# The upper feature half of the second expert, for two of four batches, goes from direct products to two added block steps; sums of x for the other two batches move into the attention

## The chip, the cores and the metric

The kernel runs on one core of a Trainium2 chip. The metric is the device time of one execution in microseconds, as the median of several executions. TensorE multiplies, VectorE, ScalarE and GpSimd work on the results, SyncE's queue issues most transfers.

## The reference

A gated linear attention gives the x of a mixture of experts, whose gate is balanced over all tokens:

```python
# q, k, v, f_logit: 4 batches, 8 heads, 768 steps, 48 wide
f = 1.0 / (1.0 + np.exp(-f_logit))
for t in range(S):
    state = f[:, :, t, :, None] * state + np.einsum('bhd,bhe->bhde', k[:, :, t], v[:, :, t])
    y[:, :, t] = np.einsum('bhd,bhde->bhe', q[:, :, t], state)
# x: y as 3072 tokens of 384; w1: 8 x 384 x 1024, w2: 8 x 1024 x 384
P = np.exp(x @ w_gate - max)
for _ in range(8):
    P /= P.sum(1, keepdims=True) + 1e-09
    P /= P.sum(0, keepdims=True) + 1e-09
    P *= N / E
for e in range(8):
    out += P[:, e:e + 1] * (np.maximum(x @ w1[e], 0.0) @ w2[e])
```

## The kernel before

Every product is made of f16 high and low parts, three matmuls for one. Tokens come in eight units u of 384; batch b holds units 2b and 2b+1. The experts are worked in two ways.

**Raw.** Experts 0 and 1 are multiplied directly. `moe(e, u, w)` makes, for each of `FT` = 8 feature tiles, nine matmuls of 384 columns into `hps`, which ScalarE turns into `hh` (relu, high part) and VectorE into `hl` (low part); then, for each of three token tiles, 24 matmuls of 384 columns into `yps`, which ScalarE copies to `yr` and SyncE writes to scratch. That is 72 + 72 matmuls for one expert and unit. `moe_tile` is the form for the first units, by token tile. Raw matmuls are TensorE's filler: `fill(n)` issues n of them between the steps of the attention (loop over g, amounts in `FILL`), and afterwards `LEAD` of them for each step of the balancing.

**The balancing** (`balance`, `sinkhorn`) is a serial chain of eight iterations, VectorE's row sums `sk_rs`, column sums `sk_cs` and products into `pe`, with one small matmul `sk_c` in each; that matmul is handed to TensorE's row `held_mm`, among the raw ones. In the same loop generators in `work` are advanced one step at a time: `convert(b)` and, from step `KSTEP` on, `prepare_w1` for the first block weights. `CONVSTEP` has the steps at which the next `convert` joins.

**Block.** Experts 2 to 7 use a scheme with fewer products: sums of blocks of x and of the weights, 15 block products for the first layer (`kb_A` to `kb_F`) and 7 for the second (`kyps`, `kxps`). A step ("period") is one entry (expert, half of the features, batch) of `ORDER`, 90 matmuls of 256 columns and 126 of 192; a group of four steps shares its weights. There are 48. `convert(b)` makes the batch's operands: three adds of high and low part (`x`), 17 sums on GpSimd (`XSUMS`, tile `xs`), copies (`XONE`), and five pieces of a split into f16 (ScalarE `xah`, `xbh`; VectorE `xal`, `xbl`). `prepare_w1` and `prepare_w2` do it for weights (`k1s` ten sums and `k2s` four on GpSimd, `k1h` and `k2h` on ScalarE, `k1l` and `k2l` on VectorE). `first_maxima`, `guard` and `verdict` look at the range of the inputs.

What sets the order: TensorE's instructions and, on VectorE, ScalarE and GpSimd, those that go through `pin` stand in the order in which the program writes them. Each engine takes its instructions in that order, and waits at the first one that isn't ready. `hps` and `yps` share four PSUM banks.

Of the kernel before, what the change touches and what calls it, by code (L numbers as in the profile page):

```python
# [1520 lines left out]
```

## Time and profile before

| | us |
|---|---|
| median of three runs | 1471.51 (1471.35 to 1471.69) |
| the profiled execution | 1472.94 |
| its span, first to last instruction | 1471.2 |
| TensorE busy | 1444.3 |
| VectorE busy | 1231.7 |
| ScalarE busy | 1061.0 |
| GpSimd busy | 1037.9 |

The profiled execution is 1.43 us above the median, and 1.74 us of it lie outside the span. Times of the trace are counted from the start of the span. The attention lasts to about 370 us, the balancing to 436, raw products to 483; then come the 48 block steps.

### The profile page before, as it was taken

The page shows a single profiled execution, that of the slowest core. Times are in us where ns is not written, and L with a number is a line of the kernel's source. Part 1 is how long each engine was busy: PE and PEld are TensorE (multiplying, and loading weights), DVE is VectorE, ACT ScalarE, POOL GpSimd, SP SyncE. Part 2 cuts the span into 40 slices and gives each one's busy share as a digit, 9 for nine tenths or more (in the row PEclk, how much of TensorE's full clock was granted, in tenths as well). Part 3 has the DMA queues.
Part 4 walks back from the last instruction along what each step waited for, and adds up shares of the span by engine and source line. Part 5 has one row for each costly group of instructions (what it writes and reads, how often), then busy time and mean ns, then how long its engine had stood idle before and what let it go on. Part 6 is the DMA issues. An engine that isn't in the chain of part 4 may idle for free.

```text
span 1471.2 us, 40349 instructions
## 1 busy us (share of the span) xinstructions
PE 1444.3 (98%) x16049; PEld 1258.5 (86%) x16049; DVE 1231.7 (84%) x2518; ACT 1061.0 (72%) x2380; POOL 1037.9 (71%) x1220
## 2 busy tenths in 40 slices
PE   7999999999999999999999999999999999999997
PEld 4788886666666799999999999999999999999996
DVE  7878888886686799888999999888888888888776
ACT  6756666664344777888888888888877787778764
POOL 2143434445457666999999999999998888888763
PEclk8999999999999999999999999999999999999999
DMA  8365455551001101222111111111111100000012
GB/s 250 101 144 136 117 126 137 130 111 55 16 34 33 49 12 29 62 61 61 56 55 53 53 57 39 48 50 55 50 34 34 34 27 30 14 20 14 2 55 79
DMA packets 107095, 92.77 MB, mean 63 GB/s; under 512 B 74160, under 2 KB 93744, under 8 KB 106896
## 3 DMA queue, kind: packets, MB, share of 16 engines
q1 hardware_dynamic: 106464, 89.51, 22.5%
q8 instruction: 127, 2.08, 0.6%
q14 instruction: 72, 0.59, 0.1%
q10 hardware_dynamic: 432, 0.59, 0.1%
HBM read 64.03 MB, written 14.16 MB: 53 GB/s over the span
## 4 chain that ended last, share of the span: by engine, by line
PE 91%; DVE 5%; ACT 2%; issue 1%; DMA 0%; POOL 0%; DVEq 0%; POOLq 0%; ACTq 0%
PE kyps L306 28%; PE yps L306 14%; PE hps L306 12%; PE kb_A L306 8%; PE kb_B L306 8%; PE kb_D L306 6%; PE kxps L306 5%; PE kb_C L306 4%; PE kb_E L306 2%; PE kb_F L306 2%; PE aps L306 1%; PE kvps L306 1%; ACT cp L1354 0%; DVE acc L1233 0%; DVE w1l L378 0%
## 5 line engine op out<-in xcount | busy, mean ns | idle before, releaser
L306 PEld LDWEIGHTS <-k1h 128*128 128x128 f16 x2880 | 270.8, 98 | 22.9 <-issue 3.9
L306 PE MATMUL kyps<-k2h,kgh 128*128 128x192 f16 x1152 | 283.4, 246 | 0.5 <-ACT kyps L1230 0.3
L306 PE MATMUL kyps<-k2l,kgh 128*128 128x192 f16 x1152 | 283.4, 246 | 0.0
L306 PE MATMUL kyps<-k2h,kgl 128*128 128x192 f16 x1152 | 283.4, 246 | 0.0
L306 PEld LDWEIGHTS <-kgh 128*128 128x128 f16 x2304 | 212.1, 98 | 7.3 <-issue 1.0
L1403 POOL TENSOR_TENSOR kgl<-kf,kgh 128x512 f16<-128x512 f32 x141 | 190.1, 1348 | 2.1 <-ACT kgh L1400 2.1
L1233 DVE SCALAR_TENSOR_TENSOR yy<-kyps,pes,part 128x192 f32<-128x192 f32 x258 | 106.5, 413 | 90.8 <-PE kyps L306 80.3
L1403 POOL TENSOR_TENSOR kgl<-kr,kgh 128x512 f16<-128x512 f32 x141 | 174.4, 1237 | 10.9 <-ACT kgh L1400 10.8
L1272 POOL TENSOR_TENSOR acc<-acc,yy 128x384 f32<-128x384 f32 x129 | 129.0, 1000 | 56.3 <-DVE yy L1233 56.3
L306 PEld LDWEIGHTS <-k1l 128*128 128x128 f16 x1440 | 140.9, 98 | 16.3
L306 PE MATMUL yps<-w2h,hl 128*128 128x384 f16 x384 | 125.3, 326 | 0.9 <-DVE hl L459 0.9
L306 PE MATMUL yps<-w2h,hh 128*128 128x384 f16 x384 | 125.3, 326 | 0.5 <-ACT hh L456 0.5
L306 PEld LDWEIGHTS <-w1h 128*128 128x128 f16 x1344 | 97.2, 98 | 33.1 <-issue 1.8
L306 PE MATMUL yps<-w2l,hh 128*128 128x384 f16 x384 | 125.3, 326 | 0.0
L306 PEld LDWEIGHTS <-kh 128*128 128x128 f16 x1152 | 108.3, 98 | 8.8 <-issue 2.5
L306 PEld LDWEIGHTS <-hh 128*128 128x128 f16 x768 | 74.1, 98 | 45.4 <-ACT hh L456 0.7
L306 PEld LDWEIGHTS <-kgl 128*128 128x128 f16 x1152 | 112.7, 98 | 0.2 <-issue 0.2
L1230 ACT ACTIVATE kyps<-kyps 128x192 f32<-128x192 f32 x144 | 45.7, 317 | 81.5 <-PE kyps L306 77.7
L1400 ACT ACTIVATE kgh<-kf 128x512 f16<-128x512 f32 x144 | 91.9, 638 | 1.0 <-DVE kf L1377 0.9
L1400 ACT ACTIVATE kgh<-kr 128x512 f16<-128x512 f32 x144 | 91.6, 636 | 0.0
L1354 ACT ACTIVATE cp<-kb_A 128x512 f32<-128x512 f32 x144 | 86.3, 599 | 3.1 <-DVE kb_A L1356 2.4
L410 DVE SCALAR_TENSOR_TENSOR hl<-hps,hh 128x384 f16<-128x384 f32 x80 | 44.0, 551 | 49.7 <-ACT hh L409 49.1
(300 smaller groups left out, 5278.1 us busy)
## 6 DMA issues: line engine op xcount, KB each, us to landing
q<-in_qkf_dram SPq DMA_DIRECT2D x23, 672.0 KB, 5.5
k1r<-in_w_dram SPq DMA_DIRECT2D x24, 384.0 KB, 3.0
ys<-yr SPq DMA_DIRECT2D x48, 192.0 KB, 2.2
k2r<-in_w_dram SPq DMA_DIRECT2D x24, 384.0 KB, 3.1
yb<-ys SPq DMA_DIRECT2D x48, 192.0 KB, 2.3
vr<-in_vc_dram SPq DMA_DIRECT2D x24, 192.0 KB, 4.9
out_dram<-acc SPq DMA_DIRECT2D x21, 192.0 KB, 1.9
w1r<-in_w_dram SPq DMA_DIRECT2D x8, 384.0 KB, 5.3
```

The lines of the kernel that those rows point to most:

```text
L306: ins = (nc.tensor.transpose if transpose else nc.tensor.matmul)(**kw)
L410: held[0] = pin(nc.vector.scalar_tensor_tensor(out=tl, in0=ps, scalar=0.0, in1=th, op0=ALU.max, op1=ALU.subtract))
L1230: pin(nc.scalar.activation(out=out, in_=in_, func=AF.Copy, **kw))
L1233: pin(nc.vector.scalar_tensor_tensor(out=y, in0=ps, scalar=p, in1=z, op0=ALU.mult, op1=ALU.add))
L1272: pin(nc.gpsimd.tensor_tensor(out=y, in0=y, in1=z.rearrange("p s d -> p (s d)"), op=ALU.add))
L1354: pin(nc.scalar.activation(out=fresh(ev[2]), in_=bk, func=AF.Copy))
L1400: pin(nc.scalar.activation(out=hs['g', t][0][i], in_=hs['f' if i else 'r', t], func=AF.Copy))
L1403: pin((nc.vector if tag == str(PERIODS - 1) else nc.gpsimd).tensor_tensor(out=hs['g', t][1][i], in0=hs['f' if i else 'r', t], in1=hs['g', ...
```

## The change

- Expert 1's upper 512 features, for the units 4 to 7 (`BLOCKED`, batches 2 and 3), are no longer raw: `features(e, u)` is 4 there and not 8. `ORDER` gets (1, 1, 2) and (1, 1, 3) at its end, a last group of two steps. The raw units are worked in the order of u, both experts for each.
- `convert` of batches 0 and 1 starts during the attention (`CONV0AT`), with its three adds on GpSimd; batch 0's is finished there, batch 1's splits come at the start of the balancing. Batches 2 and 3 join at the steps 18 and 40, with the adds on VectorE; what is left of batch 3 is spread over block step 0 (`CONVAT`), where before it was over step 1.
- `LEAD` is 7, `KSTEP` 12. An iteration of the balancing still has five steps; one small multiplication on VectorE is merged into another.
- x's maxima are not taken in `convert`: its high part is written to scratch, and `first_maxima` reads it back during the block steps. Weights in `UNSEEN` are looked at there too.
- The pools of `x32`, `xs` and the accumulators are split in two (`acca`, `accb`), and the block weights' pool opens earlier.

```diff
-RAW = [(e, u) for u in range(5) for e in range(2)] + [(0, 5), (0, 6), (0, 7), (1, 5), (1, 6), (1, 7)]
+RAW = [(e, u) for u in range(8) for e in range(2)]
+BLOCKED = (2, 3)
...
+ORDER = [(e, m, b) for e in range(2, NE) for m in range(2) for b in range(B)] + [(1, 1, b) for b in BLOCKED]
...
-LEAD = 8
+LEAD = 7
 FIRSTAT = ((0,), (1,), (0, 4), (0, 7), (1, 9), (5, 10))
 SECONDAT = ((16, 17), (18, 20), (17, 18), (17, 21), (20, 21), (20, 22), (24, 24), (23, 25))
-CONVSTEP = (26, 55, 70)
-KSTEP = 35
+CONVSTEP = (18, 40)
+KSTEP = 12
+CONV0AT = tuple(range(70, 206, 3))
...
-        yield
         pin(nc.vector.tensor_tensor(out=pe, in0=pe, in1=rs[:, :, None].to_broadcast([128, NT, NE]), op=ALU.mult))
+        yield
         pin(nc.vector.tensor_reduce(out=cs, in_=pe.rearrange("p a e -> p e a"), axis=AX.X, op=ALU.add))
         yield
         ps = psp.tile([128, NE], F32, name=f"sk_c{it}", tag=tag)
+        yield
         yield lambda: mm(out=ps, lhsT=onesf, rhs=cs, start=True, stop=True)
-        pin(nc.vector.tensor_scalar(out=cs, in0=ps, scalar1=1e-9, scalar2=None, op0=ALU.add))
+        pin(nc.vector.tensor_scalar(out=cs, in0=ps, scalar1=1e-9, scalar2=float(NE / N), op0=ALU.add, op1=ALU.mult))
         pin(nc.vector.reciprocal(out=cs, in_=cs))
-        pin(nc.vector.tensor_scalar(out=cs, in0=cs, scalar1=float(N / NE), scalar2=None, op0=ALU.mult))
-        yield
...
 
+    xscr = dp.tile([B, 128, KT, 2 * HS], F16, name="xscr")
...
+    tiles, put_off, owed = [0], [False], []
+
+    def features(e, u):
+        return FT // 2 if e and u // 2 in BLOCKED else FT
+
...
+    xc, xq = {}, []
+
+    def raw_tile(name):
+        return rp.tile([128, 768], F32, name=name, tag="wraw", bufs=3)
+
+    def convert(b):
+        xh, xl = xt[b]
+        if not all((u, t) in ready for u in (2 * b, 2 * b + 1) for t in range(TT)):
+            raise RuntimeError("a batch is not there")
+        nc.sync.dma_start(out=xscr[b], in_=xh.rearrange("p k u t -> p k (u t)"))
+        if b < 2:
+            x32 = [raw_tile(f"x32_{b}_{k}").rearrange("p (u t) -> p u t", u=2) for k in range(KT)]
+        else:
+            x32 = (acca, accb)[b % 2 == 0].tile([128, KT, 2, HS], F32, name=f"x32_{b}", tag="acc")
+            x32 = [x32[:, k] for k in range(KT)]
+        for k in range(KT):
+            pin((nc.gpsimd if b < 2 else nc.vector).tensor_tensor(out=x32[k].rearrange("p u t -> p (u t)"), in0=xh[:, k].rearrange("p u t -> p (u t)"), in1=xl[:, k].rearrange("p u t -> p (u t)"), op=ALU.add))
+            yield
...
+        yield
+        for i, (r, p, op, q) in enumerate(XSUMS):
+            pin(nc.gpsimd.tensor_tensor(out=block(r), in0=block(p), in1=block(q), op=ALU.add if op == '+' else ALU.subtract))
+            if i % 2:
+                yield
+        while b and not xq:
+            yield
+        xb = [(xq[0] if b else xq0).tile([128, 6, 256], F16, name=f"xb{n}{b}") for n in "hl"]
+        for n, (r, q, sign) in enumerate(XONE):
+            for src, dst in zip((xh, xl), xb):
+                pin(nc.scalar.activation(out=dst[:, 4 + n, :].rearrange("p (u t) -> p u t", u=2), in_=src[:, q // 3, :, 128 * (q % 3):128 * (q % 3) + 128], func=AF.Copy, scale=sign))
+            yield
+        while not {2 * b, 2 * b + 1} <= set(finished):
+            yield
+        xa = [xp.tile([128, 9, 256], F16, name=f"xa{n}{b}", tag=f"x{n}{b}", bufs=1) for n in "hl"]
...
+        if g in CONV0AT:
+            next(early, None)
         g += 1
+    for _ in converts[0]:
+        pass
...
+    work = [early]
     step, held_mm = 0, None
-    while True:
-        more = fill(LEAD * 5 / 8)
+    while fill(LEAD * 5 / 8):
         if held_mm:
             held_mm()
...
+        if not fill(LEAD * 3 / 8):
             break
         held_mm = next(chain, None)
         for gen in list(work):
@@ -1170,7 +1183,7 @@
                 work.remove(gen)
         step += 1
         if step in CONVSTEP:
-            work.append(converts[1 + CONVSTEP.index(step)])
+            work.append(converts[2 + CONVSTEP.index(step)])
...
-    at_all(1, CONVAT, converts[3])
+    at_all(0, CONVAT, converts[3])
```


Three places show how instructions move. The first is GpSimd during the balancing, where the sums of the second block weight tile (`k1s_1`) are made; `k2s_0` belongs to the first second-layer tile, `x_2` and `xs_2` to batch 2. Before:

```order
L1076 TENSOR_TENSOR k1s_1_8014<-k1r_1_8003 128x128 x2
L1076 TENSOR_TENSOR k1s_1_8014<-k1r_1_8003,k1s_1_8014 128x128
L1076 TENSOR_TENSOR k1s_1_8014<-k1s_1_8014,k1r_1_8003 128x128
L1076 TENSOR_TENSOR k1s_1_8014<-k1r_1_8003,k1s_1_8014 128x128
L1076 TENSOR_TENSOR k1s_1_8014<-k1s_1_8014 128x128
L1076 TENSOR_TENSOR k1s_1_8014<-k1r_1_8003,k1s_1_8014 128x128 x2
L1076 TENSOR_TENSOR k1s_1_8014<-k1s_1_8014,k1r_1_8003 128x128
L1076 TENSOR_TENSOR k1s_1_8014<-k1r_1_8003,k1s_1_8014 128x128
L1106 TENSOR_TENSOR k2s_0_8566<-k2r_0_8538 128x192 x2
L1109 TENSOR_TENSOR k2s_0_8566<-k2r_0_8538,k2s_0_8566 128x192 x2
L1021 TENSOR_TENSOR xs_2_8174<-x_2_8133 128x256 x2
```

With the change:

```order
L977 TENSOR_TENSOR xs_2_7671<-x_2_7626 128x256 x2
L977 TENSOR_TENSOR xs_2_7671<-xs_2_7671,x_2_7626 128x256
L977 TENSOR_TENSOR xs_2_7671<-x_2_7626 128x256
L1103 TENSOR_TENSOR k1s_1_7710<-k1r_1_7696 128x128 x2
L1135 TENSOR_TENSOR k2s_0_8194<-k2r_0_8162 128x192 x2
L1103 TENSOR_TENSOR k1s_1_7710<-k1r_1_7696,k1s_1_7710 128x128
L1138 TENSOR_TENSOR k2s_0_8194<-k2r_0_8162,k2s_0_8194 128x192
L1103 TENSOR_TENSOR k1s_1_7710<-k1s_1_7710,k1r_1_7696 128x128
L1138 TENSOR_TENSOR k2s_0_8194<-k2r_0_8162,k2s_0_8194 128x192
L1103 TENSOR_TENSOR k1s_1_7710<-k1r_1_7696,k1s_1_7710 128x128
L977 TENSOR_TENSOR xs_2_7671<-x_2_7626 128x256
L977 TENSOR_TENSOR xs_2_7671<-xs_2_7671,x_2_7626 128x256
```

The ten sums of `k1s_1` stood together and ahead of batch 2's; now the first four `xs_2` sums stand ahead of them, and the four of `k2s_0` and two more `xs_2` between them.

The second is ScalarE, where the parts of `k1h_1` stand among the evictions `hh` of a raw unit's feature tiles (the names are `hh`, unit, tile). Before:

```order
L409 ACTIVATE hh_6_0_8045<-hps_6_0_8030 128x384
L1085 ACTIVATE k1h_1_8059<-k1s_1_8014 128x640
L409 ACTIVATE hh_6_1_8063<-hps_6_1_8050 128x384
L1085 ACTIVATE k1h_1_8059<-k1s_1_8014 128x640
L409 ACTIVATE hh_6_2_8078<-hps_6_2_8067 128x384
L1085 ACTIVATE k1h_1_8059<-k1r_1_8003 128x256
L1085 ACTIVATE k1h_1_8059<-k1r_1_8003 128x384
L409 ACTIVATE hh_6_3_8094<-hps_6_3_8082 128x384
L409 ACTIVATE hh_6_4_8109<-hps_6_4_8098 128x384
```

With the change:

```order
L422 ACTIVATE hh_7_1_7759<-hps_7_1_7743 128x384
L1113 ACTIVATE k1h_1_7768<-k1s_1_7710 128x640
L422 ACTIVATE hh_7_2_7779<-hps_7_2_7763 128x384
L1113 ACTIVATE k1h_1_7768<-k1s_1_7710 128x640
L1113 ACTIVATE k1h_1_7768<-k1r_1_7696 128x256
L1113 ACTIVATE k1h_1_7768<-k1r_1_7696 128x384
L422 ACTIVATE hh_7_3_7801<-hps_7_3_7783 128x384
L985 ACTIVATE xbh_7818<-xh_4456 128x256
```

In both, `hh` of tile 3 stands behind all four parts of `k1h_1`; the unit is 6 before and 7 now.

The third is VectorE, an iteration of the balancing. Before, with the first weight tile's low parts and a batch 1 split:

```order
L155 TENSOR_REDUCE sk_cs<-pe 128x8
L1088 SCALAR_TENSOR_TENSOR k1l_0_7906<-k1s_0_7844,k1h_0_7905 128x640
L1043 TENSOR_TENSOR xal_7946<-xs_1_7715,xah_7945 128x768
L1088 SCALAR_TENSOR_TENSOR k1l_0_7906<-k1s_0_7844,k1h_0_7905 128x640
L159 TENSOR_SCALAR sk_cs<-sk_c_7957 128x8
L160 RECIPROCAL sk_cs<-sk_cs 128x8
L161 TENSOR_SCALAR sk_cs<-sk_cs 128x8
L1043 TENSOR_TENSOR xal_7946<-xs_1_7715,xah_7945 128x768
L1088 SCALAR_TENSOR_TENSOR k1l_0_7906<-k1r_0_7824,k1h_0_7905 128x256
L163 TENSOR_TENSOR pe<-pe,sk_cs 128x192
L1043 TENSOR_TENSOR xal_7946<-xs_1_7715,xah_7945 128x768
```

With the change, from the fifth `sk_c` on:

```order
L423 SCALAR_TENSOR_TENSOR hl_7_3_7802<-hps_7_3_7783,hh_7_3_7801 128x384
L163 TENSOR_SCALAR sk_cs<-sk_c_7785 128x8
L164 RECIPROCAL sk_cs<-sk_cs 128x8
L165 TENSOR_TENSOR pe<-pe,sk_cs 128x192
L1116 SCALAR_TENSOR_TENSOR k1l_1_7769<-k1s_1_7710,k1h_1_7768 128x640
L423 SCALAR_TENSOR_TENSOR hl_7_4_7826<-hps_7_4_7805,hh_7_4_7825 128x384
L153 TENSOR_REDUCE sk_rs<-pe 128x24
L154 TENSOR_SCALAR sk_rs<-sk_rs 128x24
L155 RECIPROCAL sk_rs<-sk_rs 128x24
L156 TENSOR_TENSOR pe<-pe,sk_rs 128x192
L1116 SCALAR_TENSOR_TENSOR k1l_1_7769<-k1s_1_7710,k1h_1_7768 128x640
L423 SCALAR_TENSOR_TENSOR hl_7_5_7847<-hps_7_5_7829,hh_7_5_7846 128x384
```

Before, no `hl` stands between a column sum and the next product there; now `hl_7_3`, which waits for ScalarE's `hh_7_3`, stands ahead of the eight operations that make the sixth iteration's column sum (seven are shown; the column sum is the row behind these).

On TensorE, the eight `sk_c` matmuls were 40 raw matmuls apart, and 322 raw matmuls followed the last; now they are 35 apart, and 71 follow it. Behind the second to the seventh stand 284, 248, 213, 177, 142 and 107 raw matmuls of 384 columns.

## Rows read from the trace of the kernel before

**Rows 1.** The page of the kernel before: busy us, share of the span and instructions of each engine (part 1), and the chain that ended last by engine (part 4).

```profile
PE 1444.3 (98%) x16049; PEld 1258.5 (86%) x16049; DVE 1231.7 (84%) x2518; ACT 1061.0 (72%) x2380; POOL 1037.9 (71%) x1220
...
PE 91%; DVE 5%; ACT 2%; issue 1%; DMA 0%; POOL 0%; DVEq 0%; POOLq 0%; ACTq 0%
```

**Rows 2.** Busy time by stretch of the span (start:end, length in us, then busy us and instructions of PE, PEld, DVE, ACT and POOL, granted clock, DMA share, GB/s).

```profile
220.00:400.00 180.00, 180.00 (x1996) 120.53 (x1995) 134.56 (x269) 105.18 (x230) 83.69 (x89) 1.00 0.39 93
400.00:436.00 36.00, 36.00 (x230) 22.24 (x228) 31.38 (x71) 14.96 (x30) 14.29 (x23) 1.00 0.08 29
436.00:483.00 47.00, 47.00 (x291) 28.32 (x290) 26.54 (x39) 18.42 (x39) 36.51 (x46) 1.00 0.12 38
483.00:500.00 17.00, 15.25 (x126) 11.97 (x125) 13.16 (x26) 13.81 (x28) 8.47 (x13) 1.00 0.20 59
...
540.00:640.00 100.00, 99.91 (x1069) 94.72 (x1067) 91.50 (x196) 79.24 (x183) 77.29 (x91) 1.00 0.17 45
1300.00:1400.00 100.00, 100.00 (x1072) 94.97 (x1070) 82.38 (x176) 75.81 (x176) 78.46 (x85) 1.00 0.03 10
1440.00:1472.00 32.00, 21.60 (x243) 20.18 (x241) 20.67 (x57) 11.84 (x30) 9.59 (x13) 0.90 0.23 79
```

**Rows 3.** The chain that ended last, in order of time, at the end of the raw stage (start us, length us, what).

```profile
436.63 11.70 PE hps L306 x72
...
471.74 11.70 PE yps L306 x72
```

**Rows 4.** What engines waited for between 220 and 484 us (engine, waiting work, its line, what released it: us in all, times, longest). TensorE and its weight loads have no other row in that answer.

```profile
PEld sk_m L306 <- DVE sk_r L138: 0.3, 1, 0.3
```

**Rows 5.** VectorE in order of time, one step of the Sinkhorn chain (start us, us, engine, line, operation, tiles).

```profile
425.83 0.15 DVE L159 TENSOR_SCALAR sk_cs<-sk_c 128x8 f32<-128x8 f32 x1
...
426.46 0.36 DVE L163 TENSOR_TENSOR pe<-pe,sk_cs 128x192 f32<-128x192 f32 x1
426.86 0.35 DVE L150 TENSOR_REDUCE sk_rs<-pe 128x24 f32<-128x192 f32 x1
...
427.79 0.36 DVE L154 TENSOR_TENSOR pe<-pe,sk_rs 128x192 f32<-128x192 f32 x1
428.19 0.50 DVE L155 TENSOR_REDUCE sk_cs<-pe 128x8 f32<-128x192 f32 x1
```

**Rows 6.** VectorE's groups by form between 400 and 484 us (count | busy us, mean ns of one | idle before).

```profile
L410 DVE SCALAR_TENSOR_TENSOR hl<-hps,hh 128x384 f16<-128x384 f32 x26 | 14.3, 553 | 16.8 <-ACT hh L409 16.7
L1043 DVE TENSOR_TENSOR xal<-xs,xah 128x768 f16<-128x768 f32 x8 | 8.3, 1043 | 0.6 <-ACT xah L1040 0.6
...
L1088 DVE SCALAR_TENSOR_TENSOR k1l<-k1s,k1h 128x640 f16<-128x640 f32 x4 | 3.3, 816 | 0.0
L1007 DVE TENSOR_TENSOR x<-xh,xl 128x768 f32<-128x768 f16 x3 | 2.8, 949 | 0.0
...
L1088 DVE SCALAR_TENSOR_TENSOR k1l<-k1r,k1h 128x384 f16<-128x384 f32 x2 | 1.4, 676 | 0.0
L1088 DVE SCALAR_TENSOR_TENSOR k1l<-k1r,k1h 128x256 f16<-128x256 f32 x2 | 1.1, 546 | 0.0
```

**Rows 7.** GpSimd in order of time (columns as above): the sums of a first-weight tile `k1s`, of a second-weight tile `k2s`, and of a batch of x, `xs`.

```profile
408.22 1.44 POOL L1076 TENSOR_TENSOR k1s<-k1r 128x128 f32<-128x128 f32 x2
...
414.35 0.45 POOL L1076 TENSOR_TENSOR k1s<-k1r,k1s 128x128 f32<-128x128 f32 x1
...
438.64 0.45 POOL L1076 TENSOR_TENSOR k1s<-k1r,k1s 128x128 f32<-128x128 f32 x1
439.05 1.14 POOL L1106 TENSOR_TENSOR k2s<-k2r 128x192 f32<-128x192 f32 x2
440.15 1.26 POOL L1109 TENSOR_TENSOR k2s<-k2r,k2s 128x192 f32<-128x192 f32 x2
450.94 1.41 POOL L1021 TENSOR_TENSOR xs<-x 128x256 f32<-128x256 f32 x2 [9.54 <-DVE x L1007]
...
461.87 0.73 POOL L1021 TENSOR_TENSOR xs<-x 128x256 f32<-128x256 f32 x1
...
470.25 2.84 POOL L1021 TENSOR_TENSOR xs<-x 128x256 f32<-128x256 f32 x2
```

**Rows 8.** ScalarE in order of time, weights split among the raw products' evictions.

```profile
438.52 0.73 ACT L1085 ACTIVATE k1h<-k1s 128x640 f16<-128x640 f32 x1
439.60 0.49 ACT L409 ACTIVATE hh<-hps 128x384 f16<-128x384 f32 x1 [0.35 <-PE hps L306]
...
441.45 0.82 ACT L1085 ACTIVATE k1h<-k1r 128x256 f16<-128x256 f32 x2
```

**Rows 9.** GpSimd in order of time, one tile of the attention, and TensorE's first use of what it made.

```profile
244.23 2.58 POOL L746 TENSOR_TENSOR kb<-q,kb 48x512 f16<-48x512 f32 x2 [0.37 <-ACT kb L740]
248.42 1.16 POOL L794 TENSOR_TENSOR al<-am,ah 128x512 f16<-128x512 f32 x1 [1.61 <-ACT ah L786]
249.87 0.51 POOL L758 TENSOR_TENSOR st<-carry,tds 112x192 f32<-112x192 f32 x1 [0.29 <-DVE carry L797]
...
252.93 0.40 PE L306 MATMUL yps<-al,vh 128*128 128x64 f16 x8
```

**Rows 10.** TensorE's waits between 480 and 545 us, the first block steps.

```profile
PE kb_A L306 <- ACT cp L1354: 1.4, 3, 0.8
...
PE kb_B L306 <- DVE kl L1408: 0.5, 1, 0.5
```

More of the change, by code (lines that the diff above doesn't have):

```diff
@@ L395, in moe @@
         hh, hl = [], []
-        for f in range(FT):
+        for f in range(nf):
             wh, wl = w1s[f // 2]
@@ L439, in moe_tile @@
         h = []
-        for g in range(2):
+        for g in range(nf // 4):
             ps = bank([128, 4, 128], f"hps_{e}_{u}_{t}_{g}")
@@ L468, in moe_tile @@
         n = 0
-        for f in range(FT):
-            if len(owed) > 1 - f // 4:
+        for f in range(nf):
+            if len(owed) > nf // 4 - 1 - f // 4:
                 raise RuntimeError("a low part is owed")
@@ L914, in raw_pairs @@
                     yield from moe_tile(e, u, t)
-        for e, u in pairs:
-            if u >= TILED:
+            finished.append(u)
+        for u in range(TILED, U):
+            for e in range(2):
+                if (e, u) == RAW[-1]:
+                    banks[0] += (banks[0] + features(e, u) + TT) % 2 == 0
                 yield from moe(e, u, ws[e])
-    filler, credit = raw_pairs(RAW[:-3]), [0.0]
+            finished.append(u)
+    filler, credit = raw_pairs(), [0.0]
     def fill(n):
@@ L928, in fill, with block @@
         return True
+    xc, xq = {}, []
[14 more added lines that the diff above has]
+            yield
+        sums = [(accb if b > 1 and not n else acca).tile([128, 9, 256], F32, name=f"xs{n}_{b}", tag="acc") for n in range(2)]
+        def block(v):
+            if isinstance(v, str):
+                q = int(v[1])
+                return x32[q // 3][:, :, 128 * (q % 3):128 * (q % 3) + 128]
+            n = XPOS.index(v)
+            return sums[n // 9][:, n % 9, :].rearrange("p (u t) -> p u t", u=2)
+        yield
[13 more added lines that the diff above has]
+        xa = [xp.tile([128, 9, 256], F16, name=f"xa{n}{b}", tag=f"x{n}{b}", bufs=1) for n in "hl"]
+        pieces = [(0, xa, 0, 3), (0, xa, 3, 6), (0, xa, 6, 9), (1, xb, 0, 2), (1, xb, 2, 4)]
+        for i in range(len(pieces) + 1):
+            if i < len(pieces):
+                n, dst, lo, hi = pieces[i]
+                pin(nc.scalar.activation(out=dst[0][:, lo:hi, :], in_=sums[n][:, lo:hi, :], func=AF.Copy))
+            if i:
+                n, dst, lo, hi = pieces[i - 1]
+                pin(nc.vector.tensor_tensor(out=dst[1][:, lo:hi, :], in0=sums[n][:, lo:hi, :], in1=dst[0][:, lo:hi, :], op=ALU.subtract))
+            yield
+        xc[b] = [[(xa if n < 9 else xb)[q][:, n % 9, :] for n in range(PRODUCTS)] for q in range(2)]
@@ L930, in fast @@
+    converts = [convert(b) for b in range(B)]
+    early = (x for gen in converts[:2] for x in gen)
     fixed[0] = True
@@ L1150, in fast @@
     chain = balance()
-    converts = [convert(b, left(b)) for b in range(B)]
-    work = [converts[0]]
-    kw = None
+    work = [early]
     step, held_mm = 0, None
-    while True:
-        more = fill(LEAD * 5 / 8)
+    while fill(LEAD * 5 / 8):
         if held_mm:
             held_mm()
-        more = fill(LEAD * 3 / 8)
-        if not more and kw is None:
-            wctx0.close()
-            kw = ctx.enter_context(tc.tile_pool(name="kw", bufs=4, reuse_waits="tile"))
-            filler = raws()
-            more = fill(0)
-        if not more:
+        if not fill(LEAD * 3 / 8):
             break
@@ L1185, in fast @@
                 pass
+    wctx0.close()
     wctx.close()
```

134 lines of the change are left out of this document (46 added, 88 removed).

## The prediction

> **What bounds the kernel now.** The page comes first: TensorE is busy for 1444.3 of 1471.2 us, and the chain that ended last lies on it for 91% [rows 1]. The table by stretch shows where it isn't [rows 2]. From 220 to 483 us it has no gap, and the answer on waits has no TensorE row there, only a weight load of 0.3 us [rows 4]. 1.75 us are missing in 483 to 500, at the change to the block steps, and 10.4 in the last 32 us. So fewer matmul microseconds are gained in full, if nothing else comes late. In the balancing, 400 to 436, VectorE is busy for 31.4 of 36 us, the nearest to a second bound, but the balancing ends there, and 47 us of raw products still follow: lateness costs nothing before. The change shortens this cover, so that place decides.
>
> **What TensorE loses and gains.** Each of the units 4 to 7 loses 4 feature tiles of 9 matmuls and, in each of three token tiles, 4 times 3: 72 matmuls, 288 in all. 72 take 11.70 us in the chain [rows 3], 0.1625 each: 46.8 us go. Two block steps of 90 + 126 = 216 matmuls come. A hundred microseconds of steady block steps hold 1069 and 1072 [rows 2], so a step takes 20.2 us, and two take 40.4. Net: **-6.4 us**.
>
> The weights of the added group are prepared in the group ahead, like those of the others. There TensorE shows 99.9 and 100 of 100 us beside VectorE at 82 to 92 and GpSimd at 77 to 78 [rows 2]. The twelve late reductions of x, 0.94 us each or 11 us over some 970, are hidden by TensorE too; so are the added transfers, at a DMA share of 0.03 to 0.17. Without that cover the reductions would cost those 11 us at most. The tail is the same pair of last matmuls, sums and transfer, so its 10.4 us stay.
>
> **The balancing, the term that decides.** I count from the end of the raw products as it would be without any wait (T), backwards at 0.1625 us a matmul. The second to the seventh `sk_c` then stand at T-46.1, -40.3, -34.6, -28.8, -23.1 and -17.3. Their column sums must be done by then, as TensorE waits at them with all raw work behind. VectorE needs, from [rows 5], 0.8 us from `sk_c` to the product (one operation less than there), 1.3 for row sums and their product, 0.45 for the column sum; from [rows 6], 0.5 for `hl` and 0.9 for an x add, each a little under its mean since one starts ahead of the other's end, 0.75 for a `k1l` of 640 columns, 0.6 and 0.5 for the smaller two, 0.9 for a piece of `xal`.
>
> (a) `hl` of unit 6's upper feature tile 0 ends at T-44.4 (its matmuls end at T-45.7, then 0.5 on ScalarE, a gap and 0.5). Behind it VectorE has, without a pause, the product, row sums, column sum (2.55), three `hl` (1.5), three adds of x_2 (2.6), two `k1l` (1.5) and the product after the third `sk_c` (0.8): 8.95 us. The third add ends at **T-35.5**.
>
> (b) GpSimd waits for that add and then has 4 sums of `xs_2`, 5 of `k1s_1`, 4 of `k2s_0`, 2 of `xs_2` and 5 of `k1s_1`, in that order. An `xs` takes 0.69 us (17 from 450.94 to 462.6), a `k2s` 0.6. Ten `k1s` took 5.2 us from 408.22 to 414.8 (two `xs` between them, 1.4, are taken off) and 7.2 up to 439.05, with VectorE's splits beside them [rows 7]. So 11.7 to 13.7 us; I take 12.2, near the lower end, since VectorE mostly waits meanwhile. End: **T-23.3**.
>
> (c) ScalarE has the second half of `k1h_1` and its two small parts ahead of `hh_7_3`: 0.7 + 0.8, then 0.5 for `hh` [rows 8], and 0.5 on VectorE for `hl_7_3`: **T-20.8**. TensorE's `hps_7_7` needs the bank that `hl_7_3` frees and would start at T-25.0: 4.2 us late. The row of before has this pair too, but its `k1s_1` was done long ahead, and `hh` waited 0.35 us for TensorE [rows 8].
>
> (d) Queued behind `hl_7_3` on VectorE: the sixth iteration's eight operations (2.55), two large `k1l` (1.5), two `hl` (1.0), 5.05 us: column sum at T-15.7, 7.4 late for the sixth `sk_c`. Then two small `k1l` (1.1), two `hl` (1.0), three `xal` (2.7), an `xbl` (0.65) and the seventh iteration (2.55), 8.0 us: T-7.7, **9.6 late** for the seventh. Up to the eighth, VectorE has about 5.1 us of work against 5.7 of TensorE's: no more is lost.
>
> With GpSimd at 13.7 us it is 11.1, at 11.7 it is 9.1. If (b) and (c) were not late at all, VectorE alone would be: from the fifth `sk_c` at T-28.8 it has 1.0 + 5.05 + 8.0 = 14.05 us against TensorE's 11.5 to the seventh, about 2.6. As the upper bound counts every wait, and a few operations may start ahead of those before them, I take **+9.2**.
>
> **The other places.** In block step 0, batch 3's three last pieces now stand among the first products' copies: about +2.9 us on ScalarE and +3.8 on VectorE, but batch 2's and others that stood there in steps 0 and 1 are gone. TensorE's own waits there were 1.4 and 0.5 us [rows 10]; between -1 and +2, I take 0. In the attention GpSimd gets 2 x (3 adds + 17 sums), 2 x (4.8 + 11.6) = 33 us. A tile there comes every 13 us, with GpSimd busy for 46% [rows 2]; `al` ends at 249.6 and is used at 252.9 [rows 9], a slack of 3.3 us against 1.6 for one added piece: 0, at most +3.
>
> **Sum.** 1471.2 - 6.4 + 9.2 = 1474.0 span, 1.74 outside it: 1475.7 for an execution like the profiled one. That lies 1.43 above the median, so **1474.3** against 1471.51, +0.19%. Below 0.2% (2.9 us) this kernel's change can't be told from none; the forecast is no difference, at its slower edge.
>
> **A rule weighed.** Two `xs` from 470.25 took 2.84 us where a pair at 450.94 took 1.41 [rows 7]; VectorE's splits ran beside the first. The Trainium skill, page "SBUF — State Buffer", section "Who interferes with whom", says that a VectorE instruction with two SBUF inputs and a GpSimd instruction that reads SBUF exclude each other for their whole length. The rows agree in kind. By it the six `xs` of (b), each kept waiting once, would take 4.3 us more, and the sum would be 1478.6; by the rows, with VectorE at rest in (b), it stays.
>
> **The rivals.**
> - *No wait.* GpSimd's and VectorE's lateness is taken up somewhere (the order has never run, and some 60 durations are added in a row). For it: before, TensorE never waited for the balancing, with VectorE at 87%. Against: (b) and (c) are over 4 us late by each price. 1471.51 - 6.4 = **1465.1**. Chance 0.18.
> - *VectorE alone* is late, by 2.6 to 4: **1468.2**. It needs `k1s_1` finished by T-28. Chance 0.20.
> - *My forecast*, lateness 7 to 11: 1472.1 to 1476.1. Chance 0.40.
> - *Slower: the attention comes late too.* A pair of `xs` at 1.42 each ahead of `al` and `kb` is 2.8 us; two such pairs exceed the slack of 3.3, and TensorE waits some 0.5 us in several tiles. From the point where over 3.3 us stand ahead of `al`, +3 and the balancing as forecast: **1477.3**. For it: the rows at 470.25; against: GpSimd idles over half the time there. With the same doubling in (b) instead, it would be 1478.6. Chance 0.22 for both.
>
> The range reaches from the first rival to a little above the last: 1465.0 to 1479.0; the forecast's own is 1472.1 to 1476.1. Faster by over 0.2%: the first rival, and over half of the second, 0.33. Within: the rest of it and half of the forecast, 0.29. Slower: 0.38.
>
> **What would show it.** Right: in the profile after, TensorE waits of 4 us at an `hps` for `hl` and of 2 to 4 us at two `sk_c` for `sk_cs`, 9 us together, some 15 to 35 us ahead of the first `kb_A`; GpSimd's `xs` waiting for VectorE's x; the first `kb_A` at about 446 (483.4 - 46.8 + 9.2); 50 steps at 20.2. Wrong: `kb_A` at 437 and no such rows would show the order to be free of the wait; a longer attention, or gaps in the first block steps of over 4 us, would show a loss that I put at nothing.

## The result, and the profile after

The changed kernel takes 1483.71 us (median of four, 1482.99 to 1486.24), the kernel before 1471.6 in the same comparison: ratio 1.0085, 95% interval 1.0067 to 1.0102. It is 12.1 us **slower**; forecast were 2.8, and a range up to 1479. The profiled execution took 1486.24, 13.3 above that of before, and so is its span. The page, to set beside [rows 1] (span, busy time by engine, the chain that ended last by engine):

```profile
span 1484.5 us, 40860 instructions
...
PE 1444.2 (97%) x16193; PEld 1269.4 (86%) x16193; DVE 1285.7 (87%) x2574; ACT 1087.4 (73%) x2444; POOL 1076.4 (73%) x1271
...
PE 80%; DVE 12%; ACT 3%; issue 2%; DMA 1%; POOL 1%; SPq 0%; DVEq 0%; ACTq 0%; POOLq 0%
```

TensorE's busy time is that of before, though it has 6.4 us less to do by the count; VectorE has 54 us more, and its share of the last chain went from 5% to 12%. The stretches, as in [rows 2] (length, busy us and instructions of PE, PEld, DVE, ACT, POOL, granted clock, DMA share, GB/s):

```profile
220.00:400.00 180.00, 176.02 (x1961) 116.92 (x1959) 147.19 (x264) 109.20 (x237) 83.83 (x88) 1.00 0.46 109
400.00:436.00 36.00, 28.76 (x159) 16.43 (x158) 29.80 (x63) 14.12 (x30) 20.28 (x31) 0.91 0.09 28
436.00:460.00 24.00, 23.20 (x153) 14.85 (x152) 12.33 (x25) 10.46 (x23) 12.51 (x17) 1.00 0.17 58
...
420.00:430.00 10.00, 4.49 (x22) 2.32 (x21) 8.80 (x17) 7.19 (x16) 8.05 (x10) 0.90 0.00 0
430.00:440.00 10.00, 10.00 (x49) 5.50 (x48) 8.11 (x21) 0.98 (x2) 0.00 (x0) 0.76 0.20 59
540.00:640.00 100.00, 100.00 (x1070) 94.91 (x1068) 89.59 (x190) 81.67 (x189) 84.22 (x96) 1.00 0.17 45
1240.00:1340.00 100.00, 100.00 (x1070) 94.92 (x1068) 90.92 (x185) 77.07 (x180) 82.96 (x96) 1.00 0.10 29
```

TensorE, without a gap from 220 to 483 before, now misses 4.0 us from 220 to 400, where VectorE is busy for 147 of 180 us and not 134.6, and 7.2 in the balancing. In 430 to 440 it is "busy" throughout with 49 matmuls, at a granted clock of 0.76. The steady block steps are as before.

Three marks cut the span: the first and the last gate matmul of the attention (`lps`, high part, first and last start) and the first block product (`kb_A`). Of before, then twice of after:

```profile
L306 PE MATMUL lps<-wgs,xh x72: 169/169/173, 43.5 to 368.6; 128*128 128x16 f16 x72
```

```profile
L308 PE MATMUL lps<-wgs,xh x72: 169/169/173, 43.3 to 375.8; 128*128 128x16 f16 x72
```

```profile
L308 PE MATMUL kb_A<-xbh,k1h x48: 269/272/273, 454.9 to 597.7; 128*128 128x256 f16 x48
```

| us | start to first `lps` | attention (to last `lps`) | to the first `kb_A` | to the end |
|---|---|---|---|---|
| before | 43.5 | 325.1 | 114.7 | 987.9 |
| after | 43.3 | 332.5 | 79.1 | 1029.6 |
| difference | -0.2 | +7.4 | -35.6 | +41.7 |

The attention holds as many matmuls as before (4614, 4615 before), so the 46.8 us of raw products went from the third stretch, which should then be 67.9 and is 11.2 longer; the two block steps came at 41.7. So: 41.7 - 46.8 + 7.4 + 11.2 - 0.2 = 13.3. The start differs from run to run (39.1 to 44.5 below), so the runs are compared by these stretches. Four kernels with one and the same attention gave 332.5, 332.7, 332.7 and 332.8, so half a microsecond tells there.

**The balancing** came late by the chain that the prediction had, with one stall that it didn't have and without its last one. In order of time across the engines of after; the last two lines are of the chain that ended last:

```profile
406.50 0.95 DVE L964 TENSOR_TENSOR x<-xh,xl 128x768 f32<-128x768 f16 x1
...
407.69 1.40 POOL L977 TENSOR_TENSOR xs<-x 128x256 f32<-128x256 f32 x2 [40.10 <-DVE x L964]
407.75 0.69 DVE L154 TENSOR_SCALAR sk_rs<-sk_rs 128x24 f32<-128x24 f32 x1
...
410.64 0.30 PEld L308 LDWEIGHTS sk_c<-sk_cs,onesf 128*128 128x128 f32 x2 [2.12 <-DVE sk_cs L158]
...
418.67 0.46 POOL L1103 TENSOR_TENSOR k1s<-k1r,k1s 128x128 f32<-128x128 f32 x1
...
419.16 0.74 ACT L1113 ACTIVATE k1h<-k1s 128x640 f16<-128x640 f32 x1 [2.44 <-POOL k1s L1103]
...
420.53 0.47 ACT L422 ACTIVATE hh<-hps 128x384 f16<-128x384 f32 x1
...
421.03 0.56 DVE L423 SCALAR_TENSOR_TENSOR hl<-hps,hh 128x384 f16<-128x384 f32 x1 [3.72 <-ACT hh L422]
...
422.69 1.34 DVE L1116 SCALAR_TENSOR_TENSOR k1l<-k1s,k1h 128x640 f16<-128x640 f32 x1
...
426.12 1.34 DVE L1116 SCALAR_TENSOR_TENSOR k1l<-k1s,k1h 128x640 f16<-128x640 f32 x1
...
427.85 0.48 DVE L158 TENSOR_REDUCE sk_cs<-pe 128x8 f32<-128x192 f32 x1
...
428.38 0.50 PEld L308 LDWEIGHTS sk_c<-sk_cs,onesf 128*128 128x128 f32 x2 [3.57 <-DVE sk_cs L158]
...
428.98 8.63 PE yps L308 x35
437.73 5.54 PE yps L308 x34
```

Read down: the third add of x_2 ends at 407.45; GpSimd, 40.1 us at rest, starts at once; its last `k1s_1` sum ends at 419.13; ScalarE waits for it, and `hh_7_3` ends at 421.0, VectorE's `hl_7_3`, after 3.7 us of waiting, at 421.6. The column sum is done at 428.3, and the weights of TensorE's sixth `sk_c` wait 3.6 us for it, the matmul 3.2. The stall that the prediction didn't have is the fourth `sk_c` at 410.64: beside GpSimd's first `xs_2` sums a small `sk_rs` operation took 0.69 us (0.18 before), and this matmul waited 1.7 us. TensorE's other waits here are 1.0 and 1.3 us for `hl`; the four come to 7.2 us. Behind the last of them 35 matmuls take 8.63 us where 34 take 5.54 a little later: 2.9 us more, at the lower clock. For that reason TensorE doesn't wait at the seventh `sk_c`: its column sum is done at 435.6, and TensorE comes at 437.45. The waits and the clock are 10.1 of the 11.2 us; the rest is not traced.

**The attention.** VectorE's groups by form from 140 to 355 us, before and after (count | busy us, mean ns | idle before them):

```profile
L410 DVE SCALAR_TENSOR_TENSOR hl<-hps,hh 128x384 f16<-128x384 f32 x40 | 21.9, 547 | 19.8 <-ACT hh L409 19.6
...
L753 DVE TENSOR_TENSOR ql<-q,qh 112x512 f16<-112x512 f32 x15 | 17.0, 1134 | 0.0
...
L747 DVE SCALAR_TENSOR_TENSOR vl<-vr,vh 128x384 f16<-128x384 f32 x15 | 13.3, 884 | 0.5
...
L733 DVE SCALAR_TENSOR_TENSOR q<-q,r 112x512 f32<-112x512 f32 x15 | 10.0, 664 | 0.0
...
L459 DVE SCALAR_TENSOR_TENSOR hl<-hps,hh 128x512 f16<-128x512 f32 x16 | 10.9, 683 | 12.7 <-ACT hh L456 12.5
```

```profile
L765 DVE TENSOR_TENSOR ql<-q,qh 112x512 f16<-112x512 f32 x15 | 19.9, 1324 | 0.0
L423 DVE SCALAR_TENSOR_TENSOR hl<-hps,hh 128x384 f16<-128x384 f32 x36 | 19.6, 544 | 6.1 <-ACT hh L422 5.9
L759 DVE SCALAR_TENSOR_TENSOR vl<-vr,vh 128x384 f16<-128x384 f32 x15 | 19.0, 1268 | 0.5
...
L745 DVE SCALAR_TENSOR_TENSOR q<-q,r 112x512 f32<-112x512 f32 x15 | 14.0, 931 | 0.0
...
L471 DVE SCALAR_TENSOR_TENSOR hl<-hps,hh 128x512 f16<-128x512 f32 x15 | 10.2, 677 | 7.2 <-ACT hh L468 7.2
```

`vl`, `ql` and q <- q,r have both operands in SBUF and are 43, 17 and 40% longer. The two `hl` read PSUM and are not. What TensorE waited for, from 130 to 372 us before (one row) and from 130 to 380 after:

```profile
PE yps L306 <- DVE hl L459: 0.4, 1, 0.4
```

```profile
PE yps L308 <- DVE hl L423: 2.0, 3, 0.8
PE yps L308 <- DVE hl L471: 1.7, 3, 1.3
...
PE yps L308 <- POOL al L806: 0.4, 1, 0.4
```

With two rows not shown (`sl` 0.7, `am` 0.6) it waited 5.0 us for VectorE and 0.4 for GpSimd. From the first gate matmul to the last its gaps grow by 5.1 us (7.9 against 2.8); the other 2.3 us of the 7.4 stand as busy time of the same matmuls, and the trace doesn't say why.

### The profile page after: what moved, and what is told of

Same layout as the page of the kernel before. It is cut to its first block, busy times and chain, and to the rows that moved or that the text cites. A ratio compares the mean times of both kernels' runs of the same rounds, so it can differ in the third digit from the quotient of the medians.

```text
span 1484.5 us, 40860 instructions
## 1 busy us (share of the span) xinstructions
PE 1444.2 (97%) x16193; PEld 1269.4 (86%) x16193; DVE 1285.7 (87%) x2574; ACT 1087.4 (73%) x2444; POOL 1076.4 (73%) x1271
## 4 chain that ended last, share of the span: by engine, by line
PE 80%; DVE 12%; ACT 3%; issue 2%; DMA 1%; POOL 1%; SPq 0%; DVEq 0%; ACTq 0%; POOLq 0%
PE kyps L308 29%; PE kb_A L308 8%; PE kb_B L308 8%; PE yps L308 8%; PE kb_D L308 6%; PE hps L308 5%; PE kxps L308 5%; PE kb_C L308 4%; PE kb_E L308 2%; PE kb_F L308 2%; DVE vl L759 1%; PE aps L308 1%; DVE hl L423 1%; DVE xl L833 1%; DVE sl L813 1%
## 5 line engine op out<-in xcount | busy, mean ns | idle before, releaser
L308 PEld LDWEIGHTS <-k1h 128*128 128x128 f16 x3000 | 282.3, 98 | 25.1 <-issue 5.9
L308 PE MATMUL kyps<-k2h,kgh 128*128 128x192 f16 x1200 | 295.2, 246 | 0.4 <-ACT kyps L1244 0.3
L308 PE MATMUL kyps<-k2l,kgh 128*128 128x192 f16 x1200 | 295.2, 246 | 0.0
L308 PE MATMUL kyps<-k2h,kgl 128*128 128x192 f16 x1200 | 295.2, 246 | 0.0
L1247 DVE SCALAR_TENSOR_TENSOR yy<-kyps,lg,part 128x192 f32<-128x192 f32 x270 | 111.4, 413 | 77.8 <-PE kyps L308 66.9
L308 PE MATMUL yps<-w2h,hl 128*128 128x384 f16 x336 | 110.9, 330 | 3.9 <-DVE hl L423 2.0
L308 PE MATMUL yps<-w2h,hh 128*128 128x384 f16 x336 | 111.0, 330 | 1.8 <-DVE hl L423 1.3
L308 PEld LDWEIGHTS <-w1h 128*128 128x128 f16 x1248 | 87.8, 98 | 28.1 <-issue 3.3
L308 PE MATMUL yps<-w2l,hh 128*128 128x384 f16 x336 | 110.9, 330 | 0.0
L1393 POOL TENSOR_TENSOR kr<-kr 128x256 f32<-128x256 f32 x100 | 75.9, 759 | 17.9 <-ACT kr L1382 14.8
```

Source lines behind the costliest of these rows:

```text
L308: ins = (nc.tensor.transpose if transpose else nc.tensor.matmul)(**kw)
L1247: pin(nc.vector.scalar_tensor_tensor(out=y, in0=ps, scalar=p, in1=z, op0=ALU.mult, op1=ALU.add))
L1393: pin((nc.gpsimd if ev[2] == 'P' else nc.vector).tensor_tensor(out=r[:, 0], in0=r[:, 1], in1=r[:, 0], op=ALU.subtract))
```

## The experiments

Fourteen kernels ran. All stretches (us; the time is one run or, where three or more, the median):

| kernel | attention | to `kb_A` | to the end | first `lps` to end | time |
|---|---|---|---|---|---|
| before | 325.1 | 114.7 | 987.9 | 1427.7 | 1471.6 |
| the change | 332.5 | 79.1 | 1029.6 | 1441.2 | 1483.7 |
| e1_write_only | 327.3 | 78.4 | 1029.5 | 1435.2 | 1477.2 |
| e2_late | 326.7 | 92.5 | 1030.6 | 1449.8 | 1493.4 |
| e8_reads (on before) | 325.2 | 114.6 | 987.5 | 1427.3 | 1471.2 |
| e13_reads2 (on before) | 326.5 | 114.6 | 987.6 | 1428.7 | 1472.5 |
| e14_whole | 324.7 | 138.0 | 988.0 | 1450.7 | 1491.7 |
| e4_unblocked | 334.3 | 125.1 | 988.3 | 1447.7 | 1488.6 |
| e3_ahead | 332.7 | 76.5 | 1029.2 | 1438.4 | 1483.9 |
| e5_lead8 | 332.7 | 70.5 | 1034.2 | 1437.4 | 1483.6 |
| e6_lead8_ahead | 332.8 | 71.4 | 1029.5 | 1433.7 | 1478.5 |
| e7_half | 327.8 | 75.1 | 1029.4 | 1432.3 | 1475.6 |
| e9_batch0 | 329.5 | 73.2 | 1030.1 | 1432.8 | 1478.0 |
| e10_single | 329.7 | 71.4 | 1029.4 | 1430.5 | 1475.0 |
| e11_dve | 331.4 | 71.4 | 1029.3 | 1432.1 | 1473.8 |
| e12_spread | 327.7 | 79.0 | 1029.6 | 1436.3 | 1481.4 |

**What makes the attention longer.** Theory: GpSimd's reads hold up VectorE's instructions with two operands in SBUF. Rivals: GpSimd's queue is too long ahead of `al` and `kb`; or the other work that came with the sums.

```diff
+            if b < 2:
+                pin(nc.gpsimd.memset(x32[k].rearrange("p u t -> p (u t)"), 0.0))
+                yield
+                continue
...
+            if b < 2:
+                pin(nc.gpsimd.memset(block(r), 0.0))
+            else:
```

> The changed kernel, with the adds and sums of x for batches 0 and 1 on GpSimd replaced by writes of zero to the same places: this part of the computation is left out. GpSimd keeps 40 instructions at the same places of its queue, but they read nothing. If it is the reads of GpSimd's sums that hold up VectorE's instructions with two operands in SBUF, the mean of vl in 140 to 355 us falls from 1268 to about 884 ns and of q <- q,r from 931 to about 664, the last gate matmul (lps) comes at 368 to 370 us and not at 375.9, and the time falls by 6 to 7 us. If it is the length of GpSimd's queue, or the two f16 splits of batch 0 and the write of x to scratch that lie in the attention now, the gate matmul stays at 373 to 376.

The same groups in e1_write_only, and its gate matmuls:

```profile
L423 DVE SCALAR_TENSOR_TENSOR hl<-hps,hh 128x384 f16<-128x384 f32 x38 | 20.8, 547 | 15.8 <-ACT hh L422 15.6
...
L759 DVE SCALAR_TENSOR_TENSOR vl<-vr,vh 128x384 f16<-128x384 f32 x15 | 13.9, 928 | 0.5
...
L745 DVE SCALAR_TENSOR_TENSOR q<-q,r 112x512 f32<-112x512 f32 x15 | 10.0, 664 | 0.0
```

```profile
L308 PE MATMUL lps<-wgs,xh x72: 169/169/173, 40.2 to 367.5; 128*128 128x16 f16 x72
```

`vl` is back at 928 and q <- q,r at 664, and the attention is 327.3: 5.2 of the 7.4 us go, with as many GpSimd instructions in the queue. The writes are also shorter (0.31 us each for 0.89 of a sum, 0.74 for 1.75 of an add), so this run alone doesn't exclude the queue; the waits above leave it 0.4 us, the only wait of TensorE for GpSimd there, and VectorE has none for GpSimd.

```diff
-CONV0AT = tuple(range(70, 206, 3))
+CONV0AT = ()
```

> The changed kernel, with no step of the two conversions inside the attention (CONV0AT empty): batch 0's stands right behind it, batch 1's in the balancing. All theories: the attention is as before, last gate matmul at 368 to 369 us. What the sums then cost behind it: if GpSimd is full there, the first block product comes later than now by the 30 us of sums less GpSimd's 40 us of rest, so 448 to 456 us, and the whole is 0 to 7 us faster than the changed kernel.

With no sum in it, the attention is 326.7. The whole is slower, not faster as I expected: behind the attention GpSimd doesn't keep up, and 92.5 us pass to the first block product. e1_write_only, which keeps batch 0's splits and the write of x to scratch in the attention, is only 0.6 us longer than this: the other work that came with the sums costs no more than that. But 1.6 us of the attention's loss stay. In e2_late TensorE stands still at a second product:

```profile
313.33 0.33 PE L308 MATMUL yps<-w2l,hh 128*128 128x384 f16 x1
314.24 0.34 PE L308 MATMUL yps<-w2h,hl 128*128 128x384 f16 x1 [0.58 <-DVE hl L423]
```

`hl` of the fourth feature tile is needed 11 matmuls behind the end of its `hps`, because in a halved unit the second products reach the last tile after 9 matmuls and not after 21. The disputed cost by itself, on the kernel before (e8_reads; e13_reads2 has a step of 2 for the 4):

```diff
+        if g in range(70, 206, 4):
+            pin(nc.gpsimd.tensor_tensor(out=idle[:, 0], in0=idle[:, 1], in1=idle[:, 2], op=ALU.add))
         g += 1
```

> The kernel before, with nothing of the change, and 34 added GpSimd instructions in the attention that add two operands of 256 columns from SBUF and whose result nobody uses (one each fourth g from 70 to 202; about 24 us of GpSimd). It measures the disputed cost by itself. If GpSimd's reads hold up VectorE, the mean of vl (884 ns before), q <- q,r (664) and ql (1134) rises, the attention from the first to the last gate matmul is 2 to 6 us longer than 325.1, and the time is longer by as much. If they don't, the attention stays within 1 us, since TensorE has 3.3 us of slack ahead of al.

> The kernel before with twice the idle reading GpSimd instructions of e8_reads, one each second g (68, some 47 us). e8_reads stretched ql by 17% and sl by 17%, and the attention stayed at 325.2 us, as VectorE had room. If the loss begins where VectorE's room ends, the double amount brings VectorE to 37 to 39 of 40 us in some stretches and the attention is 2 to 6 us longer than 325.1; if reads never cost TensorE anything and only the work that came with them did, it stays within 1 us.

The 34 reads made `ql` 1326 and `sl` 794 ns long (1134 and 676 before), left `vl` at 898 and q <- q,r at 664, which I expected to rise as well, and cost TensorE nothing: 325.2. So my expectation of 2 us at least was wrong. The 68 of e13_reads2, with its gate matmuls behind:

```profile
L803 DVE SCALAR_TENSOR_TENSOR sl<-st,sh 48x384 f16<-48x384 f32 x28 | 25.9, 925 | 0.3
...
L755 DVE TENSOR_TENSOR ql<-q,qh 112x512 f16<-112x512 f32 x15 | 20.1, 1339 | 0.0
...
L306 PE MATMUL lps<-wgs,xh x72: 169/169/173, 42.0 to 368.5; 128*128 128x16 f16 x72
```

1.4 us, for 59 us of reads (29 in e8_reads; GpSimd's busy time, in which some were held up themselves). Reads alone, single and evenly spread, are nearly hidden; that this is so because VectorE has room there fits, but was not tried by itself.

```diff
-BLOCKED = (2, 3)
+BLOCKED = ()
...
-CONV0AT = tuple(range(70, 206, 3))
+CONV0AT = ()
```

e4_unblocked has only the first of the two edits (in both, `ORDER` has 48 entries and `UNSEEN` the raw weights).

> The changed kernel with expert 1 raw for all units (as e4_unblocked) and no step of a conversion inside the attention (as e2_late). e2_late's attention was 1.6 us longer than before the change with no sum in it, and TensorE stood still at yps for hl of the fourth feature tile, which in a halved unit is needed 11 matmuls after its hps. If the halving is the cause, the attention here is 325 to 325.5 us; if it is the order of the units or the write of x to scratch, it stays at 326.5 or more.

```profile
L308 PE MATMUL lps<-wgs,xh x72: 169/169/173, 39.3 to 364.0; 128*128 128x16 f16 x72
```

364.0 - 39.3 = 324.7: with whole units and no sums nothing of the loss is left. The halving costs the 1.6 to 2.0 us; the new order of the units costs none. (The write of x to scratch is part of `convert` and so not in this attention.)

> The changed kernel without its first part: expert 1 stays raw for all units and the last two block steps are gone (48 steps), all else as in the change. By the count of matmuls it is 6.4 us slower than the changed kernel (46.8 us of raw products more, 40.4 of block steps less), 1490, with the same waits in attention and balancing. If the two added steps at the end cost more than their matmuls, for their weights or at the tail, it is slower by less than 4 us.

It is 1447.7 from the first gate matmul, 6.5 more than the changed kernel. That this is the counted 6.4 is in part luck: 1.8 us of it lie in the attention, and the two stretches that the count is about give 4.7 (46.0 more, 41.3 less). The attention is 334.3: with whole units the same sums cost 9.6 us (against 324.7), with halved ones 5.8 (332.5 against 326.7). The causes don't simply add; why whole units suffer more was not tried.

```diff
-            if i % 2:
+            if i % 2 or b < 2:
                 yield
...
-CONV0AT = tuple(range(70, 206, 3))
+CONV0AT = tuple(range(70, 127, 2)) + tuple(range(136, 206, 2))
```

(With `LEAD` 8, `CONVSTEP` (10, 34) and `KSTEP` 2, as in e6_lead8_ahead below; e11_dve also has the six adds on `nc.vector`.)

> e6_lead8_ahead with the sums of batches 0 and 1 still in the attention, but each in a slot of its own (one of 0.7 us instead of two, every second g), batch 1's behind a pause. If what counts is how much of VectorE's time the reads take in all, the attention stays at 332 to 333 us. If it is their bunching, and the splits of batch 0 among them, in the stretch from 220 to 300 us, it falls to 328 to 330, and the time to 1473 to 1475.

> e10_single with the six x adds of batches 0 and 1 on VectorE (0.95 us each) and not on GpSimd (1.75 each). If GpSimd's long reads cost VectorE more than the adds themselves, vl and q <- q,r fall in 140 to 355 us and the attention is 1 to 3 us shorter than in e10_single; if VectorE's own time decides, it is 1 to 2 us longer.

The same reads one by one, with a pause between the two batches: 329.7 against 332.8 in e6_lead8_ahead, so 3 us of the loss came from how they were bunched. The adds moved to VectorE cost it 1.7 more, so there VectorE's own time decides, not the length of GpSimd's add.

**What makes the balancing late.** Theory: the queue order x_2, `xs_2`, `k1s_1`, `k1h_1`, `hh_7_3`, `hl_7_3`. Rival: VectorE has too much to do for 35 matmuls a step.

```diff
-CONVSTEP = (18, 40)
-KSTEP = 12
+CONVSTEP = (10, 30)
+KSTEP = 2
```

> The changed kernel with the first block weights from step 2 of the balancing (12) and batches 2 and 3 from steps 10 and 30 (18 and 40). If the chain x_2, xs_2, k1s_1, k1h_1, hh_7_3, hl_7_3 is what makes the balancing late, hl no longer waits for hh by 3.7 us there, TensorE's two waits for sk_cs (4.9 us) and the stretch at the lower clock (76% in 430 to 440 us) go, the first block product comes 8 to 12 us earlier than 455.1, at 443 to 447, and the time is near 1473. If VectorE's own work is too much for 35 matmuls a step, 2 to 4 us of waits stay and the time is near 1476. The attention stays 7 us late by each.

From the last gate matmul to the first block product 76.5 us, only 2.6 less. What waited there (engine, work, what released it: us in all, times, longest):

```profile
POOL k1s L1103 <- DVE k1l L1116: 25.8, 1, 25.8
...
PE sk_c L308 <- DVE sk_cs L158: 3.4, 4, 2.0
...
PE yps L308 <- ACT hh L422: 1.6, 1, 1.6
```

TensorE's two waits for `sk_cs`, 4.9 us in the changed kernel, are now four with 3.4. `k1s_1` waits 25.8 us, for its buffer until `k1l_0` is through; whether this costs TensorE anything is not shown, as e6_lead8_ahead below has the same wait (27.2 us). The queue's order alone is not the cause.

```diff
-LEAD = 7
+LEAD = 8
```

> The changed kernel with 8 raw matmuls a step of the balancing, as before the change, so 40 between two sk_c and not 35 (6.5 us, not 5.7). If the balancing is late because GpSimd's chain over x_2, k1s_1 and hh holds hl_7_3 up, it stays late: hl waits for hh by 3 us or more and the first block product comes 9 us or more after the end that the raw products alone would have. If VectorE's density against 35 matmuls is the main cause, 5 us of the 11 go. The attention is as in the changed kernel.

70.5 us, 8.6 less, but the stretch behind it is 4.6 longer: with step numbers unchanged, the lateness is handed on to the first block steps, where TensorE now misses 7.2 of the first 20 us (3.5 in the changed kernel). Neither theory had that.

> Both: 8 matmuls a step, and the block weights from step 2, batches 2 and 3 from steps 10 and 34. If the queue order and VectorE's density each take their share, what is left of the balancing's lateness is under 3 us: from the last gate matmul to the first block product 68 to 71 us (79.1 in the changed kernel, 76.5 with the earlier steps alone), and the time is 1474 to 1476. If something else holds TensorE there, it stays at 75 or more.

```profile
PE sk_c L308 <- DVE sk_cs L158: 1.6, 1, 1.6
...
400.00:440.00 40.00, 37.09 (x233) 22.32 (x231) 32.71 (x73) 14.81 (x31) 24.79 (x35) 1.00 0.12 41
```

Both together: 71.4, a little over the 68 to 71 that I expected, and nothing handed on. 7.7 of the 11.2 us are gone, at a clock of 1.00 from 400 to 440; alone, the earlier steps took 2.6 and the eight matmuls 4.0 (8.6 less 4.6). So queue order and density each have a share. Of the last 3.5 us, 2.9 are two waits of TensorE, for a column sum (1.6) and for an `hl` (1.3); why they stay was not tried.

**Versions with both cured.** e7_half takes every sixth g (of the two batches, only batch 0 among the attention's tiles), `LEAD` 8, `CONVSTEP` (18, 34); e9_batch0 every fifth g with single sums, batch 1 at two steps a step, `CONVSTEP` (16, 36), `KSTEP` 8; e12_spread is e7_half with `CONVSTEP` (9, 30) and `KSTEP` 16.

```diff
-CONV0AT = tuple(range(70, 206, 3))
+CONV0AT = tuple(range(70, 206, 6))
```

> The changed kernel with only batch 0's adds and sums in the attention (every sixth step and not every third), batch 1's in the balancing, 8 matmuls a step and batch 3 from step 34. If GpSimd's reads are what slows VectorE in the attention, about half of the 7.4 us from the first to the last gate matmul remain, 328 to 330 us (325.1 before, 332.5 after); the mean of vl is near 1050 ns. What batch 1 costs in the balancing is open: 75 to 85 us to the first block product.

> The changed kernel with only batch 0's adds and sums in the attention, one instruction each fifth g; batch 1's in the balancing at two steps of its conversion a step, 8 raw matmuls a step, block weights from step 8, batches 2 and 3 from 16 and 36. By the reads theory VectorE has room for so few, and the attention is 327 to 328 us (326.7 with no sum in it); the balancing is near e6_lead8_ahead if GpSimd keeps up with batch 1 there, 70 to 74 us to the first block product, and the time is 1469 to 1474. If GpSimd doesn't keep up, 76 or more.

> The changed kernel with both losses made smaller: only batch 0's sums in the attention (every sixth step of g), 8 raw matmuls a step, batches 2 and 3 from steps 9 and 30 and the block weights from step 16, so that batch 2's sums fill GpSimd's rest of 30 us in the balancing (seen in e7_half). If reads in the attention and the queue behind x_2 are the two losses, the attention is 327 to 329 us, the first block product 70 to 72 us behind the last gate matmul (75.1 in e7_half), and the time is 1470 to 1473: about that of the kernel before. If the balancing stays at 75, something else holds it.

With one batch (e7_half) the attention is 327.8, 1.1 above e2_late, and `vl` 978 ns: a little less of both than I expected. Batch 1's adds and sums run from 345 and end at 370 already, and GpSimd rests for 30 us until x_2's adds. e9_batch0 reached the first block product as expected (73.2), but its attention is 329.5 (expected 327 to 328) and its time 1478.0 (1469 to 1474). e12_spread was to fill GpSimd's rest and failed, 79.0 and a time 0.63% above before (interval 0.46 to 0.80%):

```profile
POOL xs L977 <- ACT yr L440: 20.7, 1, 20.7
...
PE yps L308 <- DVE hl L423: 4.3, 3, 2.6
```

batch 2's first sums waited 20.7 us for something on ScalarE's side (named a `yr` copy by inference), and `hl` held TensorE at second products. No version was faster than the kernel before; the nearest is e10_single, 1430.5 against 1427.7 from the first gate matmul.

## Why the prediction was wrong, point by point

- **The count of matmuls**: right for the raw products. 41.7 and not 40.4 for the two steps; net -5.1 and not -6.4. e4_unblocked, taken back to raw products, gives 4.7 for it outside the attention.
- **The balancing, (a) to (d)**: right for the chain over four engines, not for each wait. With T at 375.8 + 67.9 = 443.7, the prediction's T-35.5, T-23.3 and T-20.8 are 408.2, 420.4 and 422.9; measured 407.45, 419.1 and 421.6. T-15.7 is 428.0, measured 428.3, though VectorE got there with two `k1l` of 1.34 us each for 0.81, beside GpSimd's sums. T-7.7, the seventh column sum, is 436.0, measured 435.6. But TensorE's waits are 7.2 us and not 9.2: 1.7 at the fourth `sk_c`, for which there was no step ("VectorE mostly waits meanwhile" is not so at 407.75), 1.0 and not 4.2 at the `hps`, none at the seventh `sk_c`. In the place of the last stands what the sum lacked, 2.9 us at the lower clock behind the stall. That 11.2 is near 9.2 is good for the chain, and luck in part for the terms.
- **The attention, "0, at most +3"**: this step failed: it measured +7.4 us. It asked whether one more GpSimd instruction fits ahead of `al`, and [rows 9] answered that. It didn't ask what the instruction does to VectorE while it runs, and that is what the runs showed in its place: 5.2 us go when GpSimd reads nothing (e1_write_only), and TensorE waits for VectorE, not for GpSimd. The rule of the Trainium skill (page "SBUF — State Buffer", section "Who interferes with whom") was quoted, and weighed for GpSimd's duration alone; it holds for both sides, and the groups of `vl` and `hl` above agree with it. The rival "attention late too" had the place, but a price from GpSimd's queue, +3, and a time of 1477.
- **The halved units**: a cost that stood in no term. That the second products of a halved unit need the last `hl` 11 and not 23 matmuls after its `hps` can be read from `moe`; 1.6 to 2.0 us of the 7.4.
- **The block steps' start, "0 between -1 and +2"**, and the hidden reductions: right. Of the 1.3 us above, 1.1 are here: in the first 40 us from the first `kb_A` TensorE misses 4.0 us, 2.9 before.
- **The range**: it was made from bounds of one decisive term. Two terms at "0" had no reach of their own. Two slips changed nothing: the seventh `sk_c` stands at T-17.4, not T-17.3, and by its own parts "within" would be 0.05 + 0.20 = 0.25 and "slower" 0.42.
